# An attention and MLP kernel: first steps in another order, a first DMA of its own, and matmul groups that are no longer interleaved

## The chip, the cores and the metric

The kernel runs on one core of a Trainium2 chip. The metric is the device time of one execution in microseconds. Of the kernel before there are three timed runs, 686.83, 687.0 and 687.04 us (median 687.0), and one profiled execution of 686.84 us, whose instructions span 685.1 us.

## The reference

Attention with 4 sink keys and a window of 128, over 4 batches of 8 heads, 768 positions and a head size of 64, and behind it an MLP with softplus:

```python
scores = scale * np.matmul(q, k.transpose(0, 1, 3, 2))
keep = is_sink | in_window          # key < n_sink, or 0 <= query - key < window
a = softmax(np.where(keep, scores, -1e9))
x = (a @ v), heads side by side     # 3072 tokens x 512
h = x @ w_in                        # 512 -> 2048
g = np.maximum(h, 0.0) + np.log1p(np.exp(-np.abs(h)))
out = g @ w_out                     # 2048 -> 512
```

The weights arrive as 64-bit floats, `n_sink` and `window` as 64-bit integers.

## The kernel before

The 3072 tokens are 12 chunks of 256. A chunk has 8 heads and 8 blocks of 256 hidden units, so the program counts in steps i = 8 * chunk + head, and a step carries one head of attention of a later chunk and one hidden block of the MLP of an earlier one. Chunks 0 and 1 take their attention products in plain fp32, in pairs of heads (`pair_scores`, `pair_weights_t`, `pair_values`); the others split each operand into a rounded high part and a remainder (`split`, `split_v`, `weights_t`) and multiply these. The MLP always does so: `up(s)` makes h from xh, xl and the two parts of w_in, 24 matmuls of 256 columns; `softplus` is three ScalarE passes; `gate` adds the positive part on VectorE and rounds the sum to gh; `residue` makes the remainder gl = t - gh; `down(s, 0, 1)` adds 12 matmuls of 512 columns to the two sums acc, two steps after `up` of the same block.

Each of the 32 half blocks of the weights goes through five stages, called w, a, c, d and l: DMA of 512 KB; a cast of the top bits (tile upper, L59 or L61 or L63); the fp32 word by shift and or on VectorE (tile wt or word_ps, L516); the high part (wi or wo, L59, L61 or L63); the remainder (wi or wo again, `_sub`, L67). Which engine does a stage is read from the strings `WT`, `WH` and `WL`, one letter for each half block (A ScalarE, V VectorE, P GpSimd); `WM` says whether the word lies in SBUF (s) or in PSUM (p), and a word in PSUM is never read by GpSimd. `NM`, `TH` and `GH` choose likewise the engine that scales the weights of a head, copies the transposed weights and makes gh.

The order of the program is written out by hand: `START` lists the first parts one by one (letter and step; S scores, T softmax, N normalise, W transposed weights, V values, O output, U up, F softplus, P gate, R residue, D and E the two halves of down, w a c d l the weights, Z matmuls on no data that only fill TensorE). TensorE and the DMA queue follow this order exactly; VectorE, ScalarE and GpSimd get their instructions in the order in which it calls them, each engine in its own queue. Behind `START` come the steps i = 17 to 105 in the order of `STEADY`: up to i = 18 the first pair of strings, from i = 19 the second, each with a variant for the first head of a chunk. From i = 19 the parts M and m take products of `up` and of `down` in turn, two and one (they are generators, so that this can be done).

The masks are made on the core (`_constants`): a DMA of 16 bytes to each partition, issued by ScalarE, brings `n_sink` and `window` (tile words); VectorE turns them into floats (L117, L118), and then VectorE, GpSimd and ScalarE make the three masks (L122 to L129).

Of the kernel before, what the change touches and what calls it, by code (L numbers as in the profile page):

```python
# [78 lines left out]
def _constants(c):  # L79

    nc, cp = c.nc, c.const
    words = cp.tile([P, 2, 2], I32, name="words")
    nc.scalar.dma_start(words[:].rearrange("p a b -> p (a b)"), c.a["sizes"].broadcast_to([P, 4]))
    room = c.ap.tile([P, 1024], F32, tag="a", name="mask_room")
    used = 0  # L90
# [30 lines left out]
    pen0, pen1 = scratch(NS), scratch(NS)  # L121
# [3 lines left out]
    nc.gpsimd.tensor_scalar(pen1, r1, c.wd, -BIG, ALU.is_lt, ALU.mult)  # L125
    nc.vector.tensor_tensor(m0[:, P:], m2[:, P:], pen0, ALU.min)
    nc.vector.tensor_scalar(m1[:, :P], fold, c.wd, -BIG, ALU.is_ge, ALU.mult)
    nc.vector.tensor_tensor(m1[:, P:], m2[:, P:], pen1, ALU.min)
    nc.scalar.copy(m2[:, :P], m1[:, :P])  # L129
# [426 lines left out]
class _Moe:  # L556
# [38 lines left out]
    def residue(self, s):  # L595
        c, nc, chunk = self.c, self.c.nc, self.chunk
        _, t = self.t.pop(s)
        gl = c.mp.tile([P, 2, CT], F32R, tag="gl", name=f"gl{chunk}_{s}", bufs=c.GB)
# [33 lines left out]
def _fast(c):  # L632
# [55 lines left out]

        return run

    def products(i, name, k, *args):
        m, s = divmod(i, H)
        if not 0 <= i < n * H:
            return iter(())
        while any(e[:2] == (s, k) for _, e in todo["l"]):
            stage("l")(i)
        return getattr(moe[m], name)(s, *args)

    def dense(*args):
        return lambda i: list(products(i, *args))  # L700

    def mixed(rest):
        def run(i):
            done, live, rounds = object(), True, 6
            if not rest:
                c.mix = products(i, "up", 0), products(i - lag, "down", 1, 0, 1)
                if (i - lag) % H == 0:
                    rounds = 0
                    for _ in range(12):
                        next(c.mix[0], None)  # L710
            up, down = c.mix
            while live and (rest or rounds):
                rounds -= 1
                got = [next(p, done) for p in (up, up, down)]
                live = any(g is not done for g in got)

        return run

# [291 lines left out]
Ctx.NM = "PPPPPAPPPAPAPPPVPAPPAPPPP"  # L1010
Ctx.TH = "VVVAAAAAAAVAAAVAAAAAAA"
Ctx.GH = "PAAAAAVVVPPPP"
Ctx.WM = "sssssssppsppssssssssssssssssssss"
Ctx.WT = "AAVAAAAAAAAAAAAPPAAAAAAAAAAAAAAV"
Ctx.WH = "APPPAAPAPPPPAAVAPAPAVAAVPAAAVAPA"
Ctx.WL = "PPPVVPPVPPVVVPVPVPPVVVPPVPPVVPPV"
Ctx.MIXED = 19
# [5 lines left out]
W0 N12 V14 V4 O4 V6 V0 S0 N6 V12 w j4 V2 N14 W14 O0 V10 N0 w w L8 O2 N2 S1 J0 w w w L10 L12 w T0 T1 S2 G4 w V8  # L1023
N1 w w w G8 w w G6 T2 L16 w w w w w G10 w L14 w w w w w w S3 T3 N3 w w w S4 T4 w W1 w k0 a a S5 T5 c c W12 w w
L18 L17 G12 W8 d K0 d a S6 T6 c l l S7 W3 a O6 O8 S8 T7 d l O12 T8 c O14 d V1 N5 N7 O1 a a c d S9 T9 c N9 k4 a
W5 V3 a Z4 S10 T10 l c c O3 Z18 S11 d K4 a a T11 l c N11 O10 l Z8 V5 O5 W7 S12 c a d d l l c d l d a c V7 O7
N4 a k8 c l p16 d d a W9 U0 F0 U1 T12 c a a d P0 S13 T13 c R0 c d d K8 G14 N13 a F1 a U2 F2 l l l V9 S14 P1 l
W11 W4 T14 G16 c l c W2 D0 a d S15 d P2 l L19 U3 a L20 T15 W13 R1 E0 c l S16 c N15 D1 O9 E1 k12 R2 E2 F3 d l d
d a a T16 D2 P3 c a U4 L22 c l l a c d N16 R3 D3 d p17 c a p18 F4 d d V11 l l a K12 c d O11 a U5 N8 l l
# [18 lines left out]

def _layout(q, k, v, n_sink, window, moe_w_in, moe_w_out):
# [30 lines left out]
```

## Time and profile before

| Part | Value |
|---|---|
| timed runs | 686.83, 687.0, 687.04 us |
| profiled execution | 686.84 us, its span 685.1 us |
| TensorE busy | 664.3 us (97%) |
| VectorE, ScalarE, GpSimd busy | 542.1, 477.9, 446.8 us |
| TensorE idle before 120 us / from 120 to 640 us | 13.8 us / none |

The profile gives for each engine the time in which it works, and for each idle time the instruction whose end released it (`<-`). PE is TensorE, PEld its weight loads, DVE VectorE, ACT ScalarE, POOL GpSimd, SP the engine that issues the DMAs. Matmuls overlap, so how fast they go is read from the starts of two rows and not from the length of one. A row of the timeline shows start, length, engine, line, operation, tiles, shapes and, in brackets, the idle time in front of it with what ended it.

### The profile page before, as it was taken

How to read it: one execution, taken by the hardware profiler on the slowest of the kernel's cores; microseconds unless marked ns; L12 is line 12 of the kernel's file. 1: busy time of each engine (PE TensorE's matmuls, PEld its weight loads, DVE VectorE, ACT ScalarE, POOL GpSimd, SP SyncE). 2: the span in 40 equal slices, each digit the busy share in tenths (PEclk: the TensorE clock that was granted, in tenths of full speed). 3: DMA queues.
4: the chain of work that ended last, by engine and by line, in shares of the span. 5: the costliest groups of instructions: out<-in, count | busy, mean ns of one | idle time of the engine just before them, and what ended most of it. 6: DMA issues, size and time to landing. Idle time of an engine off the chain costs nothing.

```text
span 685.1 us, 14176 instructions
## 1 busy us (share of the span) xinstructions
PE 664.3 (97%) x4319; PEld 592.2 (86%) x4319; DVE 542.1 (79%) x1461; ACT 477.9 (70%) x1213; POOL 446.8 (65%) x817
## 2 busy tenths in 40 slices
PE   5999989999999999999999999999999999999995
PEld 3588878999999999999999999999999999999984
DVE  6899977878888888888889888888878888753332
ACT  6999866768677677767777776777777777753331
POOL 7675479678667776795776775786866776762110
PEclk9999999999999999999999999999999999999998
DMA  8996334344344435344444434433443434310001
GB/s 311 351 404 203 103 89 126 87 116 121 102 121 125 113 90 149 97 107 117 114 117 117 125 91 110 137 107 97 131 118 92 141 93 119 100 51 1 32 1 36
DMA packets 97656, 83.33 MB, mean 122 GB/s; under 512 B 51876, under 2 KB 79140, under 8 KB 97572
## 3 DMA queue, kind: packets, MB, share of 16 engines
q1 hardware_dynamic: 97428, 82.35, 41.7%
q8 instruction: 36, 0.59, 0.4%
q14 instruction: 48, 0.39, 0.2%
q10 hardware_dynamic: 144, 0.00, 0.0%
HBM read 65.53 MB, written 16.78 MB: 120 GB/s over the span
## 4 chain that ended last, share of the span: by engine, by line
PE 83%; POOL 0%; ACT 0%; DVE 0%; POOLq 0%; issue 0%
PE acc L617 36%; PE h L574 36%; PE x L444 5%; PE s L264 3%; PE s L263 3%; PE x L438 1%; PE ts L334 0%; POOL wo L67 0%; DVE mt L590 0%; DVE o L61 0%; ACT mt L583 0%; ACT mt L584 0%; ACT mt L582 0%; POOLq L1003 0%; POOL pt L409 0%; POOL pt L406 0%
## 5 line engine op out<-in xcount | busy, mean ns | idle before, releaser
L574 PE MATMUL h<-xh,wi 128*128 128x256 f32 x1536 | 298.2, 282 | 0.3 <-DVE mt L590 0.3
L574 PEld LDWEIGHTS h<-xh,wi 128*128 128x128 f32 x1536 | 269.1, 189 | 30.1 <-issue 1.1
L617 PE MATMUL acc<-wo,gh 128*128 128x512 f32 x768 | 292.5, 395 | 1.8 <-POOL wo L67 1.2
L574 PE MATMUL h<-xl,wi 128*128 128x256 f32 x768 | 152.9, 281 | 0.0
L574 PEld LDWEIGHTS h<-xl,wi 128*128 128x128 f32 x768 | 140.2, 188 | 14.0
L617 PEld LDWEIGHTS acc<-wo,gh 128*128 128x128 f32 x768 | 143.2, 188 | 5.6 <-POOL wo L67 1.5
L617 PE MATMUL acc<-wo,gl 128*128 128x512 f32 x384 | 145.1, 393 | 1.3 <-DVE gl L67 1.3
L63 POOL TENSOR_SCALAR gh<-mt 128x512 fp32r<-128x512 f32 x88 | 54.8, 623 | 133.5 <-DVE mt L590 104.2
L582 ACT ACTIVATE mt<-h 128x512 f32<-128x512 f32 x96 | 57.6, 600 | 106.7 <-PE h L574 106.0
L590 DVE SCALAR_TENSOR_TENSOR mt<-h,mt 128x512 f32<-128x512 f32 x96 | 65.5, 683 | 35.9 <-ACT mt L584 35.9
L67 POOL TENSOR_TENSOR tl<-u,th 128x256 f32<-128x256 f32 x80 | 64.2, 802 | 45.2 <-issue 32.2
L293 ACT ACTIVATE a<-a,stats 128x136 f32<-128x136 f32 x192 | 76.0, 397 | 7.2 <-DVE stats L292 6.7
L617 PEld LDWEIGHTS acc<-wo,gl 128*128 128x128 f32 x384 | 72.3, 188 | 5.5 <-DVE gl L67 2.2
L67 DVE TENSOR_TENSOR kl<-qk,qkh 128x400 fp32r<-128x400 f32 x80 | 73.3, 916 | 2.5
L67 DVE TENSOR_TENSOR gl<-mt,gh 128x512 fp32r<-128x512 f32 x96 | 71.6, 746 | 4.1 <-POOL gh L63 4.1
L67 DVE TENSOR_TENSOR qkh<-qk,qkh 64x256 fp32r<-64x256 f32 x80 | 44.8, 560 | 27.8 <-ACT qkh L59 21.8
L318 POOL TENSOR_SCALAR a<-a,rc 128x128 f32<-128x128 f32 x156 | 58.1, 385 | 7.5 <-DVE rc L307 7.5
L583 ACT ACTIVATE mt<-mt 128x512 f32<-128x512 f32 x96 | 60.8, 633 | 3.0
L584 ACT ACTIVATE mt<-mt 128x512 f32<-128x512 f32 x96 | 60.7, 633 | 3.1
L59 ACT CAST qkh<-qk 128x656 fp32r<-128x656 f32 x80 | 59.1, 739 | 1.4 <-DMA qk<-qk 1.0
L406 POOL TENSOR_SCALAR_AFFINE_SELECT pt<-th 128x256 fp32r<-128x256 f32 x80 | 50.3, 628 | 0.0
L444 PE MATMUL x<-pt,vv 128*128 128x256 f32 (+1 forms) x216 | 47.6, 323 | 0.0
(191 smaller groups left out, 1098.2 us busy)
## 6 DMA issues: line engine op xcount, KB each, us to landing
qk<-qk SPq DMA_DIRECT2D x160, 164.0 KB, 3.1
rows<-xf SPq DMA_DIRECT2D x320, 32.0 KB, 1.6
u<-rows SPq DMA_DIRECT2D x80, 128.0 KB, 2.7
vr<-v SPq DMA_DIRECT2D x32, 192.0 KB, 2.8
out<-o SPq DMA_DIRECT2D x24, 256.0 KB, 2.3
qk<-qk SPq DMA_DIRECT2D x8, 328.0 KB, 5.7
vr<-v SPq DMA_DIRECT2D x16, 128.0 KB, 2.3
wi00r<-w SPq DMA_DIRECT2D x1, 511.8 KB, 5.8
```

The source lines that it names most:

```text
L59: nc.scalar.copy(out, in_)
L63: nc.gpsimd.tensor_scalar(out, in_, 1.0, 0.0, ALU.mult, ALU.add)
L67: (nc.vector if eng == "V" else nc.gpsimd).tensor_tensor(out, a, b, ALU.subtract)
L293: nc.scalar.activation(a, a, AF.Exp, bias=nm, scale=-1.0, accum_out=total)
L318: (nc.vector if eng == "V" else nc.gpsimd).tensor_scalar(a, a, rc[:, j : j + 1], 0.0, ALU.mult, ALU.add)
L444: nc.tensor.matmul(x[:, :, o], w, pt[:, :, m], start=False, stop=n == 2, skip_group_check=True)
L574: nc.tensor.matmul(h[:, j], wt, x, start=k == 0, stop=k >= len(prods) - 2, skip_group_check=True)
L582: nc.scalar.activation(t[:], h[:], AF.Abs)
L583: nc.scalar.activation(t[:], t[:], AF.Exp, scale=-1.0)
L584: nc.scalar.activation(t[:], t[:], AF.Ln, bias=1.0)
L590: nc.vector.scalar_tensor_tensor(t[:], h[:], 0.0, t[:], ALU.max, ALU.add)
L617: nc.tensor.matmul(self.acc[t][:], x[:, j, t * P : t * P + P], w, start=start, stop=stop, skip_group_check=True)
```

## The change

First, the two sizes, the keys of the first score tile and its queries (4, 136 and 128 words for each partition) come in one DMA of 137 KB at the head of SP's queue; the DMA of the first heads' tile leaves those keys out. Masks 1 and 2 are made after the first softmax (part m), pen0 and pen1 on VectorE, and the copy of half of mask 2 becomes an instruction of GpSimd.

Second, `START` is another list and the strings of engines are others. A new string `GL` puts the first five gl on GpSimd. Counted over the program's order, GpSimd makes 26 remainders of weights and gl in place of 16, and VectorE 102 in place of 112.

Third, from i = 19 the parts U and B take the place of M and m: all 24 products of `up`, later in the step all 12 of `down`.

```diff
-    words = cp.tile([P, 2, 2], I32, name="words")
-    nc.scalar.dma_start(words[:].rearrange("p a b -> p (a b)"), c.a["sizes"].broadcast_to([P, 4]))
+    words = c.first[:, :4].bitcast(I32).rearrange("p (a b) -> p a b", a=2)
...
+                if chunk == h == 0:
+                    lo = KW
+                    c.first = c.stg.tile([P, 4 + KW + P], F32, tag="stg", name="first")
+                    nc.sync.dma_start(c.first[:], c.a["first"])
+                nc.sync.dma_start(r[:, lo:], c.a["qk0"][chunk, h // 2, :, lo:])
...
-    nc.gpsimd.tensor_scalar(pen0, r0, c.wd, -BIG, ALU.is_lt, ALU.mult)
     nc.vector.tensor_scalar(m2[:, P:], key, c.ns, -BIG, ALU.is_ge, ALU.mult)
+    nc.vector.tensor_scalar(pen0, r0, c.wd, -BIG, ALU.is_lt, ALU.mult)
+    nc.vector.tensor_tensor(m0[:, P:], m2[:, P:], pen0, ALU.min)
     nc.vector.tensor_scalar(m0[:, :P], first, c.wd, -BIG, ALU.is_ge, ALU.mult)
+    def later():
+        nc.vector.tensor_scalar(pen1, r1, c.wd, -BIG, ALU.is_lt, ALU.mult)
+        nc.vector.tensor_scalar(m1[:, :P], fold, c.wd, -BIG, ALU.is_ge, ALU.mult)
+        nc.vector.tensor_tensor(m1[:, P:], m2[:, P:], pen1, ALU.min)
+        nc.gpsimd.tensor_scalar(m2[:, :P], fold, c.wd, -BIG, ALU.is_ge, ALU.mult)
...
-        _sub(nc, c.E["gl"], gl[:], t[:], self.g[s][0][:])
+        _sub(nc, _turn(c.GL, chunk * FP + s), gl[:], t[:], self.g[s][0][:])
...
-        "M": (mixed(False), -H),
-        "m": (mixed(True), -H),
+        "B": (dense("down", 1, 0, 1), -H - lag),
...
+Ctx.GL = "PPPPPVVVVV"
-Ctx.WL = "PPPVVPPVPPVVVPVPVPPVVVPPVPPVVPPV"
+Ctx.WL = "PPPPPPPPPPPVVPVPPVPVVPPPVPPPPPPP"
...
-    ("MYKqpmXWFSTRPNVnO", "qMSKpYWmXFTVRPONn"),
+    ("UKpFWSTRXPqNBVOYn", "WSpUKFTqBXVORPNnY"),
```

On VectorE, between the arrival of the sizes and the softmax of the first score tile (sb), stood before:

```order
L117 SCALAR_TENSOR_TENSOR words_top<-words 128x2
L118 SCALAR_TENSOR_TENSOR sizes_f<-words_top,words 128x2
L123 TENSOR_SCALAR mask_146<-mask_room,sizes_f 128x8
L124 TENSOR_SCALAR mask_144<-mask_room,sizes_f 128x128
L126 TENSOR_TENSOR mask_144<-mask_146,mask_room 128x8
L127 TENSOR_SCALAR mask_145<-mask_room,sizes_f 128x128
L128 TENSOR_TENSOR mask_145<-mask_146,mask_room 128x8
L292 ISA a_0_203,stats<-sb_0_0_171,mask_144 128x136
```

and stands now (mask 0 is number 144, mask 1 number 145):

```order
L116 SCALAR_TENSOR_TENSOR words_top<-first 128x2
L117 SCALAR_TENSOR_TENSOR sizes_f<-words_top,first 128x2
L120 TENSOR_SCALAR mask_146<-mask_room,sizes_f 128x8
L121 TENSOR_SCALAR mask_room<-mask_room,sizes_f 128x8
L122 TENSOR_TENSOR mask_144<-mask_146,mask_room 128x8
L123 TENSOR_SCALAR mask_144<-mask_room,sizes_f 128x128
L301 ISA a_0_179,stats<-sb_0_0_167,mask_144 128x136
```

Two instructions for mask 1 have left this place, and nothing in it waits for GpSimd any more.

On GpSimd, where the weights of blocks 2 to 5 are prepared, stood before (pt are transposed attention weights, gh and gl the parts of the softplus, upper, wi and wo weights):

```order
L63 TENSOR_SCALAR gh_0_669<-mt_0_625 128x512
L337 MEMSET sk_0_691 128x256
L311 TENSOR_TENSOR a_1_654<-a_1_654,rc_1_655 128x4x128
L63 TENSOR_SCALAR upper_165<-wo30r 128x512
L67 TENSOR_TENSOR wo_685<-wt_1_1_662,wo_685 128x512
L359 AFFINE_SELECT pt_2_759<-xf 128x4x128
L363 AFFINE_SELECT pt_2_759<-xf 128x4x128
L63 TENSOR_SCALAR wo_789<-wt_1_0_770 128x512
L67 TENSOR_TENSOR wi_784<-wt_0_1_683,wi_784 128x512
L359 AFFINE_SELECT pt_4_838<-xf 128x4x128
```

and stands now, from wo_672 (which was wo_685) on:

```order
L67 TENSOR_TENSOR wo_672<-wt_1_1_670,wo_672 128x512
L67 TENSOR_TENSOR wi_775<-wt_0_1_685,wi_775 128x512
L63 TENSOR_SCALAR gh_2_835<-mt_2_736 128x512
L67 TENSOR_TENSOR gl_1_837<-mt_1_728,gh_1_773 128x512
L67 TENSOR_TENSOR wo_824<-wt_1_0_763,wo_824 128x512
L368 AFFINE_SELECT pt_4_857<-xf 128x4x128
L372 AFFINE_SELECT pt_4_857<-xf 128x4x128
L67 TENSOR_TENSOR gl_2_878<-mt_2_736,gh_2_835 128x512
L67 TENSOR_TENSOR wi_876<-wt_0_0_839,wi_876 128x512
```

Between the same two pt, GpSimd has two remainders gl and one remainder wo more to make.

On TensorE, the matmuls of a step from i = 19 on began before (h is the sum of `up`, acc that of `down`, s the scores, x the values):

```order
L574 MATMUL h_4_1771<-xh_873,wi_687 128x256 x2
L617 MATMUL acc_0_1628<-wo_666,gh_2_1642 128x512
L574 MATMUL h_4_1771<-xh_873,wi_687 128x256 x2
L617 MATMUL acc_0_1628<-wo_666,gh_2_1642 128x512
L574 MATMUL h_4_1771<-xl_874,wi_687 128x256 x2
```

and now, where the scores stand behind `up` and `down` behind the scores:

```order
L583 MATMUL h_4_1770<-xh_844,wi_775 128x256 x4
L583 MATMUL h_4_1770<-xl_845,wi_775 128x256 x2
L343 MATMUL ts_1_1795<-ident,sa_1_1761 64x128
L272 MATMUL s_0_0_1819<-qkh_0_1689 128x136
L273 MATMUL s_0_0_1819<-kl_0_1692,qkh_0_1689 128x136
L272 MATMUL s_0_1_1822<-qkh_0_1689 128x264
L273 MATMUL s_0_1_1822<-kl_0_1692,qkh_0_1689 128x264
L625 MATMUL acc_0_1627<-wo_661,gh_2_1641 128x512 x2
L625 MATMUL acc_1_1628<-wo_661,gh_2_1641 128x512 x2
```

The matmuls are the same in number and shape; the scores start one group of `down` earlier in the step.

## Rows read from the trace of the kernel before

**Rows 1.** Stretches: length, busy time by engine, granted clock, DMA share, GB/s
```profile
5.00:57.00 52.00, 48.12 (x298) 34.23 (x299) 47.11 (x141) 46.76 (x132) 37.48 (x46) 1.00 1.03 384
...
20.00:85.00 65.00, 62.39 (x437) 50.10 (x434) 63.36 (x148) 59.50 (x143) 39.87 (x41) 1.00 0.77 262
41.00:91.00 50.00, 48.67 (x337) 40.97 (x336) 48.04 (x112) 45.62 (x109) 29.44 (x32) 1.00 0.57 192
...
120.00:600.00 480.00, 480.00 (x3157) 438.48 (x3156) 409.17 (x1116) 350.83 (x908) 341.92 (x652) 1.00 0.42 113
```
**Rows 2.** What TensorE waited for between 40 and 125 us: total, times, longest
```profile
PE x L438 <- DVE sk L67: 2.0, 1, 2.0
PE acc L617 <- DVE gl L67: 1.3, 2, 0.9
PE acc L617 <- POOL wo L67: 1.2, 1, 1.2
PE s L263 <- DVE stats L292: 0.5, 1, 0.5
PE h L574 <- DVE mt L590: 0.3, 1, 0.3
```
**Rows 3.** The first microseconds of VectorE in order of time
```profile
5.04 0.16 DVE L117 SCALAR_TENSOR_TENSOR words_top<-words 128x2 f32<-128x2 int32 x1 [2.52 <-DMA words<-sizes]
...
6.15 0.28 DVE L127 TENSOR_SCALAR mask<-mask_room,sizes_f 128x128 f32<-128x128 f32 x1
6.38 0.17 DVE L128 TENSOR_TENSOR mask<-mask,mask_room 128x8 f32<-128x8 f32 x1
6.50 0.30 DVE L292 CUSTOM_DVE_ANT_0 a<-sb,mask 128x136 f32<-128x136 f32 x1
```
**Rows 4.** The first matmul of TensorE
```profile
4.88 0.83 PE L246 MATMUL sb<-qk 64*128 64x136 f32 x4 [4.88 <-DMA qk<-qk]
```
**Rows 5.** GpSimd's remainders before 110 us: busy us, mean ns, idle before
```profile
L67 POOL TENSOR_TENSOR wi<-wt,wi 128x512 fp32r<-128x512 f32 x9 | 14.2, 1580 | 2.2 <-DMA rows<-xf 1.9
L67 POOL TENSOR_TENSOR wo<-wt,wo 128x512 fp32r<-128x512 f32 x7 | 10.5, 1495 | 2.2 <-ACT wo L59 2.0
```
**Rows 6.** VectorE's remainders before 110 us, and kl over the span (min/median/max)
```profile
L67 DVE TENSOR_TENSOR gl<-mt,gh 128x512 fp32r<-128x512 f32 x9 | 6.9, 764 | 0.0
L67 DVE TENSOR_TENSOR wo<-wt,wo 128x512 fp32r<-128x512 f32 x8 | 5.4, 682 | 0.0
...
L67 DVE TENSOR_TENSOR kl<-qk,qkh x80: 574/999/1285, 39.4 to 594.2; 128x400 fp32r<-128x400 f32 x80
```
**Rows 7.** TensorE in order of time: first rows of groups, and of what follows them
```profile
67.64 0.72 PE L574 MATMUL h<-xh,wi 128*128 128x256 f32 x4
...
70.59 0.29 PE L263 MATMUL s<-qkh 128*128 128x264 f32 x1
...
89.89 0.63 PE L617 MATMUL acc<-wo,gh 128*128 128x512 f32 x2
...
92.65 0.27 PE L334 MATMUL ts<-ident,sa 128*64 128x128 f32 x1
...
99.51 0.64 PE L574 MATMUL h<-xh,wi 128*128 128x256 f32 x4
...
102.39 0.29 PE L263 MATMUL s<-qkh 128*128 128x264 f32 x1
...
301.58 0.39 PE L574 MATMUL h<-xh,wi 128*128 128x256 f32 x2
...
307.18 0.23 PE L263 MATMUL s<-qkh 128*128 128x136 f32 x1
...
354.38 0.40 PE L574 MATMUL h<-xh,wi 128*128 128x256 f32 x2
...
360.01 0.28 PE L263 MATMUL s<-qkh 128*128 128x264 f32 x1
```
**Rows 8.** The last matmuls in order of time
```profile
675.64 2.11 PE L617 MATMUL acc<-wo,gh 128*128 128x512 f32 x8 [0.56 <-POOL gh L63]
```

More of the change, by code (lines that the diff above doesn't have):

```diff
@@ L95, in scratch @@
         return room[:, used - n : used]
-    rel, key, lt, fold, first, r0, r1 = (scratch(n) for n in (P, NS, P, P, P, NS, NS))
+    rel, key, lt, fold, first, r0, r1, pen0, pen1 = (scratch(n) for n in (P, NS, P, P, P, NS, NS, NS, NS))
     nc.gpsimd.iota(rel, pattern=[[-1, P]], base=0, channel_multiplier=1, allow_small_or_imprecise_dtypes=True)
@@ L120, in _constants @@
     m0, m1, m2 = c.masks = [cp.tile([P, KW], F32, name=f"mask{i}") for i in range(3)]
-    pen0, pen1 = scratch(NS), scratch(NS)
-    nc.gpsimd.tensor_scalar(pen0, r0, c.wd, -BIG, ALU.is_lt, ALU.mult)
     nc.vector.tensor_scalar(m2[:, P:], key, c.ns, -BIG, ALU.is_ge, ALU.mult)
+    nc.vector.tensor_scalar(pen0, r0, c.wd, -BIG, ALU.is_lt, ALU.mult)
+    nc.vector.tensor_tensor(m0[:, P:], m2[:, P:], pen0, ALU.min)
     nc.vector.tensor_scalar(m0[:, :P], first, c.wd, -BIG, ALU.is_ge, ALU.mult)
[L125 to L129, printed above, removed]
+    def later():
[3 more added lines that the diff above has]
+        nc.gpsimd.tensor_scalar(m2[:, :P], fold, c.wd, -BIG, ALU.is_ge, ALU.mult)
+    c.later_masks = later
 class _Attention:
@@ L194, in load @@
                 r = c.lp.tile([P, QK], F32, tag=("qk", "qkh")[h // 2 % 2], name=f"qk{chunk}_{h}")
-                nc.sync.dma_start(r[:], c.a["qk0"][chunk, h // 2])
+                lo = 0
+                if chunk == h == 0:
[3 more added lines that the diff above has]
+                nc.sync.dma_start(r[:, lo:], c.a["qk0"][chunk, h // 2, :, lo:])
                 self.heads[h] = r
@@ L244, in pair_scores @@
             rows = slice(e * D, e * D + D)
-            q = r[rows, KC + j * P : KC + j * P + P]
-            nc.tensor.matmul(s[:, e, :w], q, r[rows, j * KW : j * KW + w], start=True, stop=True)
+            q, k = r[rows, KC + j * P : KC + j * P + P], r[rows, j * KW : j * KW + w]
+            if chunk == h == j == 0:
+                q, k = c.first[rows, 4 + KW :], c.first[rows, 4 : 4 + KW]
+            nc.tensor.matmul(s[:, e, :w], q, k, start=True, stop=True)
     def scores(self, h):
@@ L619, in down @@
             )
-            yield
         if last:
@@ L689, in stage, with dense @@
         return run
[L691 to L702, printed above, removed]
-        def run(i):
[L704 to L715, printed above, removed]
+    def dense(name, k, *args):
+        def run(i):
+            m, s = divmod(i, H)
+            if 0 <= i < n * H:
+                while any(e[:2] == (s, k) for _, e in todo["l"]):
+                    stage("l")(i)
+                getattr(moe[m], name)(s, *args)
         return run
@@ L771, in _fast @@
         "w": (dma, 0),
+        "m": (lambda i: c.later_masks(), 0),
         **{kind: (stage(kind), 0) for kind in "acdl"},
@@ L791, in _fast @@
         for i in range(2 * H + 1, (n + 1) * H + lag + 1):
-            for part in "JjGLx" + c.STEADY[i >= c.MIXED][i % H == 0]:
+            for part in "JjGLx" + c.STEADY[i >= c.JOINED][i % H == 0]:
                 run, ahead = parts[part]
@@ L948, in _general @@
                 for s in range(FP):
-                    list(m.up(s))
+                    m.up(s)
                     m.softplus(s)
@@ L953, in _general @@
                     for j in range(2):
-                        list(m.down(s, j))
+                        m.down(s, j)
 def _kernel(tc, a, out):
@@ L960, in _kernel @@
     c.nc, c.tc, c.a, c.out = nc, tc, a, out
-    c.E = dict(qkh="A", ql="V", kl="V", vh="A", vl="P", xh="A", xl="P", gl="V", tl="P", out="AV")
+    c.E = dict(qkh="A", ql="V", kl="V", vh="A", vl="P", xh="A", xl="P", tl="P", out="AV")
     c.x, c.vs, c.vsr, c.vsh = {}, {}, {}, {}
@@ L1009 @@
 Ctx.GB, Ctx.EXACT = 3, 2
[L1010 to L1015, printed above, removed]
-Ctx.WL = "PPPVVPPVPPVVVPVPVPPVVVPPVPPVVPPV"
-Ctx.MIXED = 19
+Ctx.NM = "APPPAVVPVPAAAPAAPVPAVVPPAP"
+Ctx.TH = "AVAAAAVAAAAAVAAAAAAAVVA"
+Ctx.GH = "PAPAAAVVVPPVPP"
+Ctx.GL = "PPPPPVVVVV"
+Ctx.WM = "sssppssspsppssssssssssssssssssss"
+Ctx.WT = "AAPAAAAAAAAAPAAPPAAAAAAAPAAPAAAA"
@@ L1018 @@
+Ctx.WH = "AAVVAPPAPAPAPAVAVAAAPPAAPAAPVPVA"
+Ctx.WL = "PPPPPPPPPPPVVPVPPVPVVPPPVPPPPPPP"
+Ctx.JOINED = 19
 Ctx.STEADY = (
     ("kWUqYpKSFTXRDVPONE", "SWTkpUKERDNFXPqYVO"),
-    ("MYKqpmXWFSTRPNVnO", "qMSKpYWmXFTVRPONn"),
+    ("UKpFWSTRXPqNBVOYn", "WSpUKFTqBXVORPNnY"),
 )
 Ctx.START = """
-W0 N12 V14 V4 O4 V6 V0 S0 N6 V12 w j4 V2 N14 W14 O0 V10 N0 w w L8 O2 N2 S1 J0 w w w L10 L12 w T0 T1 S2 G4 w V8
-N1 w w w G8 w w G6 T2 L16 w w w w w G10 w L14 w w w w w w S3 T3 N3 w w w S4 T4 w W1 w k0 a a S5 T5 c c W12 w w
@@ L1025 @@
[L1025 to L1029, printed above, removed]
@@ L1030 @@
-S17 F5 c T17 P4 c W10 l R4 p19 V13 O13 W15 X16 a a d S18 l a U6 E3 d T18 D4 P5 d c S19 T19 R5 l l d c p20 F6 q16 l
-l P6 N18 N17 J16 x16 E4 V15 X17 L21 G18 a O15 U7 x17 N19 S20 W16 c c c U8 D5 E5 F7 X18 k16 N10 T20 x18 R6 F8 P7 X19 R7 P8 K16 E6 d d d p21
-a D6 N20 W17 V16 W6 l l O16
+S0 N12 W12 V14 w V12 w w V10 W0 S1 T0 m j4 N2 N14 T1 w O0 L8 w w V2 O2 w L12 w S2 L10 w O4 G8 G4 N0 V6 w W14 w
+N1 L16 V0 L14 G6 w w S3 V4 w w N6 w T2 w J0 w w T3 N3 a a S4 V8 L17 w w S5 T4 w W1 k0 G10 T5 K0 w w S6 w W8 O8 c
@@ new lines @@
+c d w a w l w S7 T6 W3 a S8 O12 w d w c G12 l T7 T8 c d L18 d V1 N5 O1 N7 l w a a S9 V3 c a T9 c N9 k4 W5 S10
+O14 d a T10 d l c O3 c Z4 a K4 a d S11 T11 N4 l O6 c N11 O10 l Z18 W7 V5 O5 a l c d d c l Z8 k8 l S12 a V7 a d w
+c d O7 p16 W9 a U0 U1 l F0 T12 d c d a P0 S13 c d T13 a c L20 c K8 G16 R0 N13 U2 L19 F1 l a d F2 l W11 W4 a V9 l
+S14 c T14 W2 a P1 d l l D0 E0 c a S15 U3 d d l T15 P2 R1 c l c O9 N15 W13 a F3 S16 a d R2 k12 d T16 P3 c l l c
+G14 l d U4 a L22 d a c R3 c N16 p18 F4 a l p17 d V11 a c O11 B1 N8 K12 d l U5 B2 S17 l F5 T17 d P4 c l R4 V13 a
@@ L1033 @@
+l c O13 p19 W15 a S18 a d P5 T18 l d d l a U6 D3 E3 S19 c T19 X16 d l c N18 x16 p20 D4 E4 V15 R5 q16 N17 c l F6
+W16 L21 d U7 l X17 W10 G18 P6 O15 c F7 R6 J16 W6 S20 X18 d U8 B5 x17 N19 F8 x18 T20 N10 k16 P7 R7 K16 P8 a W17
+X19 N20 l l D6 E6 p21 V16 d O16 a c
 """
@@ L1046, in _blocks, with _first @@
     return w.view(np.int64) if w.dtype == np.float64 else w
+def _first(qk, n_sink, window):
+    words = np.array([n_sink, window], np.int64).view(np.float32)
+    r = qk[0, 0, :2].reshape(P, QK)
+    return np.concatenate([np.broadcast_to(words, (P, 4)), r[:, :KW], r[:, KC : KC + P]], axis=1)
 def _layout(q, k, v, n_sink, window, moe_w_in, moe_w_out):
@@ L1065, in _layout @@
         "vs": np.ascontiguousarray(v[:, :, :NS].reshape(B, 2, G * NS, D).transpose(0, 2, 1, 3)),
-        "sizes": np.array([n_sink, window], np.int64).view(np.int32).reshape(1, 4),
+        "first": _first(qk, n_sink, window),
         "w": _blocks(moe_w_in, moe_w_out),
```

1 line of the change is left out of this document (removed).

## The prediction

> **What bounds the kernel now.** I read the busy table by stretches first, then TensorE's list of waits, then the timeline where either pointed. From 120 to 600 us TensorE works in every one of 480.00 us, and its granted clock is 1.00, the higher of its two levels (2.4 GHz) [rows 1]. There no other engine can shorten the time; only the matmuls' own spacing can. What another order can win lies before 120 us, where TensorE idles, and at the end. From 20 to 85 us VectorE works 63.36 of 65.00 us and ScalarE 59.50, while GpSimd works 39.87 [rows 1]: there the preparation of the weights and the first two chunks' softmax pace the program, and TensorE, which follows its written order, stands whenever VectorE is late. Its waits between 40 and 125 us are 2.0 us for the remainder of the sink weights, 1.3 for gl, 0.5 for a score buffer, 0.3 for a softplus buffer, all released by VectorE, and 1.2 for a weight remainder of GpSimd: 5.3 us together [rows 2]. Before that come 4.88 us until the first keys land [rows 4], and at the end 0.56 us for a gh [rows 8].
>
> **The first DMA and the masks.** VectorE is done with what needs no sizes and idles 2.52 us until they arrive at 5.04 [rows 3]; TensorE's keys arrive at 4.88 [rows 4]. Now both need the one transfer at the head of SP's queue, 137 KB in place of 328 KB and without a second queue beside it. What it gains has two ends. At least nothing: the 2 KB of sizes came no earlier than the 328 KB of keys, so size may not be what counts. At most 2.5 us, all of VectorE's idle time. I take 1.0, nearer to nothing, because two transfers that differ so much in size landed within 0.2 us. The two instructions for mask 1 that stood between 6.15 and 6.50 [rows 3] go behind the first softmax, which gives that one another 0.35 us and takes it from the next. The rest of the first heads' tile is now second in the queue and lands about when the whole did; it is needed one score tile later. VectorE's queue thus starts 1.0 us earlier; of that I let 0.7 reach TensorE at 40 us, since ScalarE and the transfers of weights follow their own pace. The early waits of TensorE on GpSimd and VectorE between 5 and 40 us, in an order that changes little there, I leave as they are, with 1.5 us of doubt to either side.
>
> **The remainders.** Ten remainders leave VectorE for GpSimd: five gl at 0.764 and five of weights at about 0.682 us [rows 6] are 7.2 us; against them VectorE gets some casts and scalings back, together about 1.2 us by the counts of the order and the lengths of like rows. So VectorE has 6.0 us less before TensorE leaves this stretch. In 41 to 91 us it worked 48.04 of 50.00 [rows 1]; it would work 42 of them. The four waits that VectorE released, 2.0 + 1.3 + 0.5 + 0.3 = 4.1 us, each came when it was late by less than these 6 us, so I let them go, at -4.1. The 1.2 us wait on GpSimd's wo came at 104 us, behind the stretch in which it will be fuller; the order now has that remainder well ahead of its use, so it goes too, at -1.2.
>
> On GpSimd the ten cost more, 5 x 1.50 for gl (no row has gl there; I take the 1.495 of wo, whose form is the same), 2 x 1.580 for wi and 3 x 1.495 for wo [rows 5]: 15.1 us. In 41 to 91 us it worked 29.44 of 50 us [rows 1], so 20.6 us were free and 5.4 us stay free: it would be busy for 89% of the stretch. That is the weak point. The queue is in order, and what stands behind a gl is a transposed weight (pt) or a wi remainder for which TensorE waits. Most of its idle time was spent waiting for ScalarE and VectorE, and those waits do not vanish because the queue is longer. TensorE's new waits on GpSimd are therefore at least nothing and at most what went, 5.3 us, or more if it falls behind for good; I take 2.0, more than one remainder of 1.5 us that stands too late.
>
> VectorE operations with two inputs in SBUF get longer beside GpSimd: kl takes 574 ns at best and 999 at the median [rows 6]. The Trainium skill (SBUF — State Buffer, section SBUF: two separate sides) says why: VectorE and GpSimd share one pair of ports, which one of them holds for its whole instruction while the other stands still. By the rows a remainder on GpSimd costs VectorE up to 0.43 us, if it meets such an operation. The skill speaks of a full stop for as long as the other works; by that rule each could cost 1.5 us and VectorE would lose all 6 us again. The spread of kl, 0.4 and not 1.5 us, says that it is seldom so much.
>
> **The groups.** From i = 19 two matmuls of `up` and one of `down` alternated; a step's 24 and 12 took 307.18 - 301.58 = 5.60 us or 360.01 - 354.38 = 5.63 [rows 7]. Apart, as the first steps have them, the 24 took 102.39 - 99.51 = 2.88 and the 12 took 92.65 - 89.89 = 2.76: 5.64 us [rows 7]. That is 0.01 to 0.04 more in each of the 85 steps, 0.9 to 3.4 us; not below nothing by these rows, though 1 us of it is within what the starts can tell. I take +1.0. The worst row is 70.59 - 67.64 = 2.95 for the 24 [rows 7], behind a half-array matmul, which the later steps don't have in front of `up`.
>
> The grouping has a second effect, at the end. The last `up` comes 2.76 us earlier within its step, with 24 matmuls of `down` (5.5 us) behind it, so softplus and gh of the last block are ready; the 0.56 us [rows 8] go, at -0.5.
>
> **Sum.** -0.7 - 4.1 - 1.2 + 2.0 + 1.0 - 0.5 = -3.5 us against the profiled execution of 686.84, 683.3 us. The median of the runs is 687.0, 0.16 above, so the forecast may stand for either at that precision.
>
> **Rivals.** First, GpSimd becomes the bound. For it speaks the 89%; against it that its work is needed by TensorE only in some places, each some microseconds ahead. If its waits reach the 5.3 us that went, the time is 683.3 + 3.3 = 686.6; the skill's rule of the full stop (it gives VectorE back its 6 us) would come out there as well. It spans 685.4 to 687.
>
> Second, slower: the groups. If each `up` took 2.95 as in its worst row, a step would take 2.95 + 2.76 = 5.71, 0.09 more than the middle of 5.60 and 5.63, and 85 steps cost 7.6 in place of 1.0 us: 689.9. It decides once a step loses 0.05 us (4.5 us over 85 steps eat the rest). For it speaks that the steps are where TensorE never idles, so nothing hides it; against it that the one run of 24 in the neighbourhood of the later steps took 2.88.
>
> Third, no change: the transfers pace the first 57 us. From 5 to 57 us the DMA engines are busy throughout (share 1.04) [rows 1], so work that is ready sooner could find its weights not there. Against it, no wait of TensorE behind its first names a transfer [rows 2]. Then the waits come back as waits for weights, and the 0.5 us at the end and about as much before it are won against 1.0 us lost on the groups: 686.8, spanning 686.2 to 687.4.
>
> **How the numbers follow.** Forecast 0.58, its own range 681.0 to 685.4 (new waits 0 to 4, first transfer 0 to 2). GpSimd 0.20, groups 0.10, transfers 0.12. About 0.2%, 1.4 us, is what a measurement of this kernel can tell from no change: below 685.6 is faster, above 688.4 slower. Faster: 0.57 of the first case, 0.12 of the GpSimd case, 0.01 of the third, 0.70. Slower: the groups' 0.10 and 0.02 of GpSimd falling behind for good, 0.12. Same: 0.18. The range from 679.8 (all doubts on the good side: the early waits too) to 687.6 leaves out the groups and little else.
>
> **What would show it.** Right: TensorE's first matmul at about 3.9 us; the waits for sk and gl gone; GpSimd near 44 busy in 50 us between 41 and 91 us; no idle TensorE behind 120 us; the first step with i = 19 some 4 us earlier. Wrong: waits of TensorE on GpSimd's wi, wo or pt of over 4 us together; 24 `up` in 2.95 us; idle TensorE in the steps, where the scores now come 2.76 us earlier; or a first matmul at 4.9 us.

## The result and the profile after

The changed kernel takes 693.3 us (median of 4 runs, 692.3 to 693.7) against 687.0 us beside it: a ratio of 1.0088, with a 95% interval of 1.0075 to 1.0101. It is 6.2 us slower where 683.3 us, 3.7 less, was forecast, and outside the range (679.8 to 687.6). Its profiled execution took 692.32 us, the span 690.6 us.

The loss lies before 105 us. The first row of the values of step 16 (x from the rounded sink weights) has the same 547 matmuls in front of it in both traces, of before and of after. It stands at:

```profile
98.85 0.35 PE L438 MATMUL x<-sk,vs 128*128 128x256 f32 x1 [2.04 <-DVE sk L67]
```

```profile
104.40 0.36 PE L447 MATMUL x<-sk,vs 128*128 128x256 f32 x1
```

That is 5.55 us late. From there on, by the starts of the same row in each step, it stays between 5.2 and 5.8 us, and falls slowly from the one to the other: 5.8 us in the first steps, 5.2 in the last. The stretches of after, which answer to [rows 1]; the columns are again the length, then TensorE, weight loads, VectorE, ScalarE, GpSimd, granted clock, DMA share and GB/s:

```profile
41.00:91.00 50.00, 45.19 (x283) 36.79 (x284) 47.94 (x93) 39.94 (x96) 41.42 (x40) 0.93 0.59 189
...
75.00:80.00 5.00, 4.14 (x19) 2.82 (x20) 5.00 (x12) 4.60 (x11) 5.00 (x4) 0.50 0.43 116
...
120.00:600.00 480.00, 480.00 (x3160) 440.88 (x3159) 392.54 (x1125) 347.45 (x911) 331.46 (x650) 1.00 0.42 115
```

VectorE issues 93 instructions from 41 to 91 us where it issued 112, and is as busy as before: 47.94 us against 48.04. That is the row to stop at. GpSimd took 12.0 us more, 41.42 of 50. TensorE works 3.5 us less than in [rows 1], and part of that at half clock: 0.50, the lower level (1.2 GHz), from 75 to 80 us. From 120 us on TensorE works without a pause, as before.

TensorE's waits between 40 and 125 us, which answer to [rows 2] (total us, times, longest):

```profile
PE s L273 <- DVE kl L67: 1.7, 2, 1.1
PE x L428 <- DVE xl L67: 1.5, 1, 1.5
PE s L272 <- DVE qkh L67: 0.9, 1, 0.9
PE h L583 <- POOL wi L67: 0.7, 1, 0.7
PE h L583 <- DVE wi L67: 0.5, 1, 0.5
PE acc L625 <- DVE wi L67: 0.4, 1, 0.4
PE h L583 <- DVE mt L598: 0.4, 1, 0.4
PE s L272 <- DVE stats L301: 0.3, 1, 0.3
```

The waits for sk and gl are gone. In their place TensorE has 6.4 us of other waits: 5.0 for other remainders of VectorE, 0.7 for its mt and stats, and 0.7 for GpSimd.

Why VectorE is as busy with 19 instructions fewer shows in its rows, here in order of time (start, length, shapes and, in brackets, idle time):

```profile
58.50 0.41 DVE L67 TENSOR_TENSOR xl<-x,xh 128x256 fp32r<-128x256 f32 x1
...
60.21 1.30 DVE L332 TENSOR_TENSOR sa<-a,rc 128x64 f32<-128x64 f32 x1
...
62.26 0.68 DVE L598 SCALAR_TENSOR_TENSOR mt<-h,mt 128x512 f32<-128x512 f32 x1
62.87 1.56 DVE L525 SCALAR_TENSOR_TENSOR wt<-wo40r,upper 128x512 int32<-128x512 int32 x1
64.34 1.76 DVE L67 TENSOR_TENSOR wo<-wt,wo 128x512 fp32r<-128x512 f32 x1
...
73.62 1.76 DVE L525 SCALAR_TENSOR_TENSOR wt<-wo50r,upper 128x512 int32<-128x512 int32 x1
...
77.07 0.67 DVE L525 SCALAR_TENSOR_TENSOR wt<-wo51r,upper 128x512 int32<-128x512 int32 x1
77.67 1.76 DVE L67 TENSOR_TENSOR wo<-wt,wo 128x512 fp32r<-128x512 f32 x1
```

and beside it GpSimd's:

```profile
58.01 1.73 POOL L67 TENSOR_TENSOR gl<-mt,gh 128x512 fp32r<-128x512 f32 x1
59.70 1.72 POOL L67 TENSOR_TENSOR wo<-wt,wo 128x512 fp32r<-128x512 f32 x1
...
62.57 1.30 POOL L67 TENSOR_TENSOR gl<-mt,gh 128x512 fp32r<-128x512 f32 x1
63.84 1.72 POOL L67 TENSOR_TENSOR wi<-wt,wi 128x512 fp32r<-128x512 f32 x1
...
73.52 1.31 POOL L67 TENSOR_TENSOR wo<-wt,wo 128x512 fp32r<-128x512 f32 x1
74.78 1.73 POOL L67 TENSOR_TENSOR wi<-wt,wi 128x512 fp32r<-128x512 f32 x1
...
77.07 1.81 POOL L67 TENSOR_TENSOR wi<-wt,wi 128x512 fp32r<-128x512 f32 x1
```

The shift and or (wt) takes 0.67 us at 77.07 and 1.76 at 73.62, where a remainder of GpSimd has started just before it; a subtraction takes 0.68 [rows 6] and 1.76: 1.08 us more each. The xl at 58.50, one of whose inputs (x) lies in PSUM, takes its 0.41 us in the middle of a remainder of GpSimd. GpSimd's own row grows too, from 1.30 to 1.72, and to 1.81 at 77.07, where both engines start together and wt is the one that keeps its length. I will call this a hold.

Over all of VectorE's instructions that start before 104 us, I took as a hold's length what an instruction takes beyond the shortest of the same operation, tiles and shape (in any of the 17 kernels here), and counted those with over 0.3 us. The lengths are summed row by row, and rows overlap a little, so the sum can exceed the 104 us:

| kernel | instructions | sum of their lengths, us | held | their excess us |
|---|---|---|---|---|
| before | 244 | 105.0 | 13 | 8.0 |
| after | 229 | 107.8 | 30 | 21.9 |

### The profile page after: what moved, and what is told of

The parts are those of the page before. It is cut to its first block, busy times and chain, and to the rows that moved or that the text cites. A ratio compares the mean times of both kernels' runs of the same rounds, so it can differ in the third digit from the quotient of the medians.

```text
span 690.6 us, 14197 instructions
## 1 busy us (share of the span) xinstructions
PE 668.2 (97%) x4319; PEld 597.8 (87%) x4319; DVE 532.9 (77%) x1461; ACT 471.3 (68%) x1206; POOL 452.9 (66%) x824
## 4 chain that ended last, share of the span: by engine, by line
PE 85%; DVE 3%; ACT 1%; issue 1%; DMA 0%; SPq 0%; DVEq 0%; ACTq 0%
PE h L583 36%; PE acc L625 36%; PE x L453 5%; PE s L273 3%; PE s L272 3%; PE x L447 1%; DVE kl L67 1%; DVE wt L525 0%; DVE qkh L67 0%; DVE wo L67 0%; PE ts L343 0%; DVE a L327 0%; PE x L435 0%; DVE wo L61 0%; DMA rows<-xf 0%
## 5 line engine op out<-in xcount | busy, mean ns | idle before, releaser
L583 PE MATMUL h<-xh,wi 128*128 128x256 f32 x1536 | 247.0, 283 | 1.6 <-POOL wi L67 0.7
L583 PEld LDWEIGHTS h<-xh,wi 128*128 128x128 f32 x1536 | 211.5, 191 | 6.7 <-POOL wi L67 0.9
L625 PE MATMUL acc<-wo,gh 128*128 128x512 f32 x768 | 196.3, 394 | 0.4 <-DVE wi L67 0.4
L625 PEld LDWEIGHTS acc<-wo,gh 128*128 128x128 f32 x768 | 137.7, 188 | 26.0 <-DVE wi L67 0.9
L67 POOL TENSOR_TENSOR tl<-u,th 128x256 f32<-128x256 f32 x80 | 70.2, 877 | 127.7 <-issue 116.4
L583 PEld LDWEIGHTS h<-xl,wi 128*128 128x128 f32 x768 | 119.7, 192 | 0.0
L625 PE MATMUL acc<-wo,gl 128*128 128x512 f32 x384 | 105.9, 390 | 0.0
L327 POOL TENSOR_SCALAR a<-a,rc 128x128 f32<-128x128 f32 x150 | 63.4, 436 | 2.0 <-DVE rc L316 2.0
L67 DVE TENSOR_TENSOR kl<-qk,qkh 128x400 fp32r<-128x400 f32 x80 | 54.9, 687 | 2.3
L473 DVE TENSOR_TENSOR xt<-x,xt 64x256 f32<-64x256 f32 x80 | 33.0, 412 | 30.3 <-ACT xt L59 30.0
```

What stands on the lines that cost most here:

```text
L67: (nc.vector if eng == "V" else nc.gpsimd).tensor_tensor(out, a, b, ALU.subtract)
L327: (nc.vector if eng == "V" else nc.gpsimd).tensor_scalar(a, a, rc[:, j : j + 1], 0.0, ALU.mult, ALU.add)
L625: nc.tensor.matmul(self.acc[t][:], x[:, j, t * P : t * P + P], w, start=start, stop=stop, skip_group_check=True)
```

## The experiments

**What does not cost.** The groups alone, the kernel before with U and B from i = 19:

```diff
+        "B": (dense("down", 1, 0, 1), -H - lag),
...
-    ("MYKqpmXWFSTRPNVnO", "qMSKpYWmXFTVRPONn"),
+    ("UKpFWSTRXPqNBVOYn", "WSpUKFTqBXVORPNnY"),
```

> The kernel before with one part of the change alone: from i = 19 the 24 products of up and the 12 of down in groups. Theory C, groups: a step gets 0.01 to 0.09 us longer and the time rises by 1 to 7 us. Rival: the distance between the two profiles shrinks from 5.75 to 5.17 us over the steps and the end, so the groups are worth -0.6 us, 686.4.

686.57 us, ratio 0.9992 (0.9983 to 1.0002): no cost can be seen. In the changed kernel's trace, which answers to [rows 7], the 24 of `up` start at 300.56 and what follows them at 303.42; the 12 of `down` at 303.89, the next at 306.63:

```profile
300.56 0.63 PE L583 MATMUL h<-xh,wi 128*128 128x256 f32 x4
...
303.42 0.23 PE L272 MATMUL s<-qkh 128*128 128x136 f32 x1
...
303.89 2.00 PE L625 MATMUL acc<-wo,gh 128*128 128x512 f32 x8
...
306.63 0.28 PE L447 MATMUL x<-sk,vs 128*128 128x256 f32 x1
```

2.86 + 2.74 = 5.60 us, what it was interleaved.

Nor is the new order what costs most. The changed kernel with the old `START` (part m behind T0), everything else new:

> The changed kernel with the list of first steps of the kernel before (mask 1 and 2 made between T0 and T1); the engine strings, the first DMA and the groups stay changed. Theory A, ports: GpSimd's ten extra remainders hold up VectorE's two-input operations, whatever the order; the time stays above the 687.0 us of before, 689 to 694. Theory B, order: the new list is what makes VectorE's results late; with the old list the time falls to 685 to 687.

696.29 us, ratio 1.0128 (1.0111 to 1.0145): 3 us slower still, above both ranges. With the new order and the old strings (GL on VectorE; only `WM` stays new):

```diff
-Ctx.WL = "PPPPPPPPPPPVVPVPPVPVVPPPVPPPPPPP"
+Ctx.WL = "PPPVVPPVPPVVVPVPVPPVVVPPVPPVVPPV"
-Ctx.GL = "PPPPPVVVVV"
+Ctx.GL = "V"
...
```

> The changed kernel, its new list of first steps kept, with the engine strings NM, TH, GH, WT, WH and WL of the kernel before and all gl on VectorE. Theory A, ports: without the ten extra remainders on GpSimd VectorE's operations are short again and the time falls by 3 to 6 us, to 687 to 690. Theory B, order: the list was made for the other strings or is bad by itself; the time stays at 692 or goes above.

688.59 us, ratio 1.0020 (1.0009 to 1.0031). In the new order the strings cost 4.7 us of the 6.2. Undoing one half of the move each (only `GL`, only `WL`):

> The changed kernel with all gl on VectorE again (five remainders fewer on GpSimd, between 45 and 85 us). Theory A: each of the five holds VectorE's shift-and-or or subtraction for about 1 us, and costs it 0.76 us if done there itself; so VectorE gains 1 to 2 us net and TensorE with it, and the stalls at 72 to 77 us shrink with the half-rate stretch behind them: 688 to 691 us, against 693.3. Rival B (GpSimd's queue is the bound): more, 687 to 689. Rival C (VectorE's own load decides, and each operation moved to it costs its 0.76 us): 694 to 697.

> The changed kernel with the weight remainders spread over the engines as before (five fewer on GpSimd; the gl stay there). Theory A: half of what the ten cost, as much as the five gl gave back (1.5 us) or a little more: 690 to 692. If the weight remainders on GpSimd were the good part of the move: 693 to 696.

691.79 and 691.48 us (1.0048 to 1.0079, 1.0042 to 1.0076): 1.5 and 1.8 us back, either half about as dear (the first a little less than my theory asked for). Together that is 3.3 of the 4.7 us; what the other strings cost was not tried alone.

**Hold or queue?** GpSimd's 26 remainders are replaced by zero fills, which read nothing from SBUF:

```diff
-def _sub(nc, eng, out, a, b):
+def _sub(nc, eng, out, a, b, fill=False):
+    if fill and eng == "P":
+        for _ in range(3):
+            nc.gpsimd.memset(out.bitcast(F32), 0.0)
+        return
...
```

The remainders of weights and gl call it with `fill`; their share of the result is left out.

> The changed kernel in which each remainder of weights and gl that GpSimd makes (26 of them) is three fills with zero, about as long (3 x 0.5 us) but without reading SBUF; these remainders' products are then left out of the sums. Theory A, ports: VectorE no longer stands still, its 1.76 us shift-and-or goes back to 0.7 us, and the time falls below 687, to 682 to 686. Rival B2, the queue: GpSimd's queue is as long as before and the time stays at 691 to 693.

680.08 us, ratio 0.9902 (0.9885 to 0.9919), below even the range of the ports, with GpSimd fuller than in the changed kernel (46.95 us from 41 to 91). But a fill doesn't wait for its inputs. So a subtraction of 8 columns was put in front, and the two together are the stand-in of a remainder:

```diff
+        nc.gpsimd.tensor_tensor(out[:, :1, :8], a[:, :1, :8], b[:, :1, :8], ALU.subtract)
         for _ in range(3):
```

> The changed kernel, each of GpSimd's 26 remainders replaced by a subtraction of 8 columns (so it still waits for the same inputs and still stands in the same place of the queue) and three fills of its output with zeros, which take about as long together as the remainder did; the products of those remainders are left out of the result. It controls the run with fills alone (680.1 us), whose fills wait for nothing. Theory A (a remainder of GpSimd holds up VectorE's instructions that read two SBUF inputs, the fills do not): 680 to 683 us, wt from wir or wor at about 0.7 to 0.85 us. Rival B (what costs the time is that GpSimd's queue is long and waits for inputs, in order): 688 to 693 us. In between: both.

687.10 us, ratio 0.9999 (0.9990 to 1.0008): between the theories. VectorE was busy for only 38.24 us from 41 to 91, but a stand-in now took 2.12 us on the mean, and TensorE waited 3.1 us at 67.6 us for one. Even so, with stand-ins longer than the remainders, it is 6.2 us faster than the changed kernel. With two fills, a stand-in takes 1.57 us on the mean and a remainder of the changed kernel 1.49:

> As the run with the 8-column subtraction and fills (687.1 us), but two fills in place of three: each stand-in then takes about 1.5 us on GpSimd, as the remainder of the changed kernel does where nothing hinders it, while the former took 2.1 to 2.3. The products of the 26 remainders are left out of the result. The prediction had VectorE lose nothing to GpSimd's remainders but TensorE wait 2 us on GpSimd; if that was right but for the hold, its 683.3 us should come out here: 681.5 to 685.5. Rival (what the former run lost was not the length of the stand-in but the waits for inputs in a queue in order): 686 to 687.5, as before.

681.30 us, ratio 0.9911 (0.9894 to 0.9927). From 41 to 91 us, and all that TensorE waited for from 40 to 125 us:

```profile
41.00:91.00 50.00, 49.00 (x340) 41.27 (x339) 43.99 (x108) 44.04 (x107) 45.87 (x81) 1.00 0.67 210
...
PE x L433 <- ACT wi L59: 0.4, 1, 0.4
PE h L588 <- POOL wi L70: 0.4, 1, 0.4
PE s L278 <- DVE kl L72: 0.2, 1, 0.2
```

GpSimd works 45.87 of 50 us, more than in the changed kernel, in the same order and behind the same inputs, and TensorE waits 0.4 us for it. VectorE does 15 instructions more in 4 us less. Neighbouring rows of the two engines there, VectorE's first:

```profile
62.57 0.69 DVE L530 SCALAR_TENSOR_TENSOR wt<-wo41r,upper 128x512 int32<-128x512 int32 x1 [1.43 <-POOL wi L68]
63.18 0.68 DVE L72 TENSOR_TENSOR wi<-wt,wi 128x512 fp32r<-128x512 f32 x1
63.78 1.10 DVE L530 SCALAR_TENSOR_TENSOR wt<-wi60r,upper 128x512 int32<-128x512 int32 x1
```

```profile
62.59 1.11 POOL L70 MEMSET wi<- 128x512 f32 x2
63.68 1.68 POOL L63 TENSOR_SCALAR wo<-wt 128x512 fp32r<-128x512 f32 x2
```

Beside fills wt and the subtraction take 0.69 and 0.68; beside a GpSimd operation that reads SBUF (wo from wt) wt is held again, 1.10. So what costs is that GpSimd's remainders read SBUF: 12.0 us of the changed kernel's time hang on that. Counted as in the table, 11 instructions are still held here, for 5.0 us, beside other operations of GpSimd. The same stand-ins in the kernel before (16 of them):

> The kernel before, each of its 16 remainders on GpSimd replaced by a subtraction of 8 columns and two fills (products of those remainders left out of the result). In the changed kernel the same replacement took 12.0 us away, for 26 remainders, 0.46 us each. If the hold is proportional to their number, 16 x 0.46 = 7.4 us go here, to about 679.7: then the change's ten account for 4.6 us of its loss. If the hold was cheap before (few of the 16 met an operation of VectorE for which TensorE waits), 683 to 686: then the change's loss of 6.2 us is all of it new hold. If it was as dear before as after (675 to 677), the loss lies in something else than the hold.

685.28 us, ratio 0.9973 (0.9963 to 0.9984), 1.9 us. The holds by the remainders cost 1.9 us before the change and 12.0 after it. Without them the change would have been worth 681.30 - 685.28 = -4.0 us.

**More of one thing in the old order.** Only the five gl of the kernel before go to GpSimd:

> The kernel before, in its own order, with only one thing changed: the first five gl are made on GpSimd. VectorE has 5 x 0.764 = 3.8 us less to do between 42 and 90 us, GpSimd has 5 x 1.3 to 1.7 us more and was busy 29 of 50 us there. By the prediction's reasoning the time falls by 1 to 3 us, to 684 to 686. By theory A (each remainder on GpSimd holds up a two-input operation of VectorE by about 1.1 us) VectorE loses more than it is given: 687.5 to 690. If gl's place in the order hides both: 686.5 to 687.5.

692.92 us, ratio 1.0087 (1.0070 to 1.0104), more than any theory of mine. Here it is in the main not the hold. GpSimd:

```profile
56.17 0.97 POOL L359 TENSOR_SCALAR_AFFINE_SELECT pt<-xf 128x512 f32<-128x512 f32 x1 [0.85 <-ACT xf L59]
57.09 1.08 POOL L363 TENSOR_SCALAR_AFFINE_SELECT pt<-xf 128x512 f32<-128x512 f32 x1
58.15 2.50 POOL L67 TENSOR_TENSOR gl<-mt,gh 128x512 fp32r<-128x512 f32 x2
```

and TensorE:

```profile
59.46 0.50 PE L617 MATMUL acc<-wo,gl 128*128 128x512 f32 x1 [2.50 <-POOL gl L67]
...
60.77 1.06 PE L617 MATMUL acc<-wo,gh 128*128 128x512 f32 x2
...
64.13 0.62 PE L617 MATMUL acc<-wo,gh 128*128 128x512 f32 x2
```

gl stands behind two selects, and the old order needs it at once; behind the wait two matmuls take 1.06 us in place of 0.62, at the lower clock (granted 0.52 from 60 to 63 us). With stand-ins for these five gl:

> The kernel before with the first five gl on GpSimd (692.9 us), these five replaced by a subtraction of 8 columns and two fills (products of those gl left out). Its trace shows TensorE waiting 2.50 and 1.39 us for gl itself, which stands on GpSimd behind two selects of pt, and 3 us at half clock behind the first wait; VectorE stood idle beside. If these waits in GpSimd's queue are the price: 691 to 693.5. If the hold is: 5 x 0.46 = 2.3 us less or more, 688 to 690.6.

691.14 us (1.0045 to 1.0076): at most 1.8 us of the 5.8 are holds (the intervals of the two runs just overlap), the rest is the queue; the longest wait for gl is still 2.6 us. The changed order makes gl ahead of its use, and its trace has no wait for gl.

**The clock.** The changed kernel with 28 matmuls on no data at three places where it waits:

> The changed kernel with 28 matmuls on no data (376 columns) put at three places where TensorE waits, ahead of the parts V3, S17 and V13, so that TensorE does not stand there. Theory: behind the stalls at 72 to 77 us the granted clock falls to its lower level and the matmuls of the next 6 us take twice as long, which costs about 2.8 us of the 6.2 us by which the changed kernel is slower; with the clock kept up the time falls by 2 to 3 us, to 690 to 691. Rival: VectorE would be as late all the same and TensorE merely waits instead of working slowly, no gain (692 to 694), or more where the matmuls on no data run over the stall.

692.46 us, ratio 1.0078 (1.0062 to 1.0093), not to be told from 1.0088. Its row for the half-clock stretch:

```profile
75.00:80.00 5.00, 5.00 (x46) 4.36 (x45) 5.00 (x11) 4.94 (x12) 5.00 (x4) 1.00 0.44 126
```

The clock was kept at 1.00, and TensorE then waited 2.9 us for an mt of VectorE at 96.4 us. The slow stretch is a consequence of the waits, and without it VectorE was as late; my 2.8 us for it are not borne out.

**Fewer, and the rest.** The first DMA and the groups on the old order and strings:

> The kernel before with the first DMA and its masks, and with the groups of U and B from i = 19, but with the old order of the first steps and the old strings (16 remainders on GpSimd). The remainders are what costs the time, the first DMA brings the first matmul from 4.88 to about 3.2 us, and the groups cost nothing: 684.5 to 686.3 us, faster than both kernels by 0.1 to 0.4 per cent. Rival: what is won at the first matmul is lost before 40 us, since weights and ScalarE pace the work there: 686.3 to 687.2.

685.95 us, ratio 0.9984 (0.9975 to 0.9993): a little faster than both kernels. Against it the new order with the old strings (688.59, `WM` apart) is 2.6 us slower, while with the new strings it was 3.0 us faster than the old (693.26 against 696.29): order and strings have no price apart from each other. With every second remainder of GpSimd's 16 on VectorE besides:

> The kernel with the old order, the new first DMA and the groups (685.95 us), and every second weight remainder that GpSimd has there moved to VectorE: 9 in place of 16 or so stay on GpSimd, VectorE has 7 to 8 x 0.68 = about 5 us more of its own. Theory A at its strongest (a remainder on GpSimd costs VectorE 1.1 us, on VectorE itself 0.68): 682 to 685.5. Rival (VectorE, which works 63 of 65 us there, is the bound by its own load, and the holds met only some of its operations): 687 to 691.

690.43 us (1.0026 to 1.0059), so my theory at its strongest falls: VectorE's own load counts as well, and in the old order 16 on GpSimd is better than 9, or than 26 (696.29, where the other strings are new too). And with part K16 moved ahead of F8 and P7:

> The kernel with the old order, the new first DMA and the groups (685.95 us), with one part of the first steps earlier: K16, the copy and remainder of the sink weights, stands ahead of F8 and P7 in place of behind P8. TensorE waits 2.00 us at 98.4 us for that remainder, which stands on VectorE behind two casts, a gl and two sums mt. If nothing else is late there: 1 to 1.9 us faster, 684.1 to 685. If the next late operation (gl or gh, which go 0.6 us later) takes the place of the wait: 685.3 to 686.5.

686.92 us (0.9985 to 1.0006), no gain, and 1.0 us more than without that move. The wait for sk is gone and another has come:

```profile
PE acc L626 <- POOL wo L67: 3.1, 1, 3.1
```

## Why the prediction was wrong

**The step that failed** is in the part on the remainders: "a remainder on GpSimd costs VectorE up to 0.43 us", from the spread of kl, by which a full stop "is seldom so much", and with it the 6.0 us of relief: the sum has no term for what the ten cost VectorE. A hold takes 1.08 us at a wt or a subtraction, 0.73 on the mean of the 30 counted (21.9 / 30). The ten remainders took about 7 us from VectorE, and by the table holds grew by 21.9 - 8.0 = 13.9 us. Even the row that I used says more than 0.43: its longest kl, 1285 ns, is 0.71 us above its best [rows 6]. And the trace of before had the dearer row, outside the one operation that I looked at:

```profile
53.04 1.77 DVE L516 SCALAR_TENSOR_TENSOR wt<-wi50r,upper 128x512 int32<-128x512 int32 x1
...
52.66 1.61 POOL L67 TENSOR_TENSOR wi<-wt,wi 128x512 fp32r<-128x512 f32 x1
```

The Trainium skill (SBUF — State Buffer, section SBUF: two separate sides) calls the shared ports an exclusive lock for the whole instruction; a VectorE operation with two SBUF inputs meets it only against a GpSimd operation that reads SBUF, one in a two-port mode against any. On the two inputs the traces agree: 1.76 beside a remainder, 0.68 beside a fill. I named the rule and priced it by the wrong row. Even the rival with the full stop (686.6) was too low: it let VectorE lose its 6 us, but by the count of held instructions it lost more than twice that.

None of the signs that the prediction named for being wrong came: the waits on GpSimd were 0.7 us, the 24 of `up` took 2.86 at 300 us, TensorE had no idle time from 120 to 600 us, and the first matmul stood at 3.14. The signs looked at TensorE and GpSimd; none looked at the length of VectorE's rows. The rival with the transfers didn't come either: between 40 and 125 us no wait of TensorE names one (the share that it gives as 1.04 is 1.03 in [rows 1]).

**TensorE's waits on GpSimd, +2.0.** Measured 0.7. GpSimd was busy 41.4 of 50 us, not 44.5, and was not the bound; with the remainders' holds gone it could be busy 45.9 and cost 0.4. Lengthened to 2.1 us a piece, it did become the bound (687.1).

**The four waits, -4.1, and wo, -1.2.** They went, and 6.4 us of others came, since VectorE was later, not earlier. Without the remainders' holds all but 1.0 us of waits go and the change wins 4.0 us, near the 3.5 of my sum: the rest of the working held, as far as that run can tell, its stand-ins being only like remainders in length.

**The first DMA, -0.7.** Better than thought at its place, which answers to [rows 4] and [rows 3]:

```profile
3.14 0.83 PE L255 MATMUL sb<-first 64*128 64x136 f32 x4 [3.14 <-DMA first<-first]
```

```profile
3.12 0.18 DVE L116 SCALAR_TENSOR_TENSOR words_top<-first 128x2 f32<-128x2 int32 x1 [0.60 <-DMA first<-first]
...
4.52 0.30 DVE L301 CUSTOM_DVE_ANT_0 a<-sb,mask 128x136 f32<-128x136 f32 x1
```

1.74 us earlier at TensorE, 1.98 at the first softmax; I had 1.0. That the 2 KB and the 328 KB landed together did not mean that size is nothing: the 137 KB landed 1.74 us earlier than the 328 KB did. Whether the size or the second queue counted, no run tells apart. What reaches the end is less: with the groups it was worth 1.2 us in the old order.

**The groups, +1.0.** No cost can be measured. The rows of [rows 7] that differed by 0.04 us were within what starts can tell. That the lateness falls from 5.8 to 5.2 us over the steps speaks rather for a gain of some 0.6; the run with the groups alone (0.4 us less) can't confirm it. **The end, -0.5:** no idle time in front of the last block's `down`, which answers to [rows 8]:

```profile
680.10 1.98 PE L625 MATMUL acc<-wo,gh 128*128 128x512 f32 x8
```

What stays open: how the 12 us divide between waits and the lower clock, and why the first 40 us win nothing from an earlier start in the changed order. By the starts of the same score matmuls the lead of 1.74 us has become a lag of 1.1 us by 24.5 us, and 0.9 by 41 us; a shift and or held for 1.78 us stands at 18.9 us, but that it is the cause is not shown.

## What to carry to other kernels

Before moving an elementwise operation from VectorE to GpSimd, list VectorE's operations whose inputs all lie in SBUF and read their longest row, not one operation's median; each that meets a GpSimd operation reading SBUF can pay up to that much. Busy time that stays the same while the count of instructions falls is a sign. Whether an engine off the path bounds anything can be tried with stand-ins of equal length that wait for the same inputs but read next to nothing.

## What was not expected of the hardware

An operation with a single SBUF input is held too: VectorE's cast of wt to wo, 0.42 us alone, took 1.10 us on the mean of three in the changed kernel. Such a cast can be held even beside a fill, which left the subtraction alone. In the kernel with three fills and no subtraction in front:

```profile
50.76 0.85 DVE L61 CAST wo<-wt 128x512 fp32r<-128x512 f32 x1
```

```profile
49.64 1.69 POOL L69 MEMSET wo<- 128x512 f32 x3
```

So the stand-ins take away the holds of operations with two SBUF inputs, not all of them. An operation with one of its two inputs in PSUM was not held, even wholly inside GpSimd's remainders:

```profile
36.32 0.68 DVE L67 TENSOR_TENSOR wo<-word_ps,wo 128x512 fp32r<-128x512 f32 x1
```

```profile
34.60 2.97 POOL L67 TENSOR_TENSOR wi<-wt,wi 128x512 fp32r<-128x512 f32 x2
```

Waits of 0.9, 0.5 and 1.5 us within 3.0 us (72.8 to 75.9) were followed by some 6 us of matmuls at the lower clock; two matmuls of x from sk that took 0.59 us before took 1.19.
